# Gated mix of two linear-attention blocks on one core: the gate column made by VectorE, one block of copies moved to ScalarE

## The chip, the core and the metric

The kernel runs on one core of a Trainium2 chip. The time is the device time of one execution in microseconds, the median of several runs. The profile comes from one further execution. In it PE is TensorE, PEld TensorE's weight loads, DVE VectorE, ACT ScalarE, POOL GpSimd, and SP the engine that here only issues DMAs.

## The reference

Two linear-attention blocks, A and B, work on the same x (2048 x 640, bf16) with weights of their own, and a gate per row mixes them. Cut to what matters:

```python
x = A_x
g = sigmoid((x * gate_w).sum(-1, keepdims=True))
a = block(x, A_wqkv, A_wo)
b = block(x, B_wqkv, B_wo)
return g * a + (1 - g) * b

def block(x, wqkv, wo):              # 32 heads of 20
    q, k, v = split(x @ wqkv)
    pq, pk = phi(q), phi(k)          # phi(t) = (t + 1 if t > 0 else exp(t)) + 1e-6
    kv, z = pk.T @ v, pk.sum(rows)   # per head
    return ((pq @ kv) / (pq @ z + 1e-6)) @ wo
```

The row sums behind the gate are a matrix product of x with one column, gate_w. The kernel takes them from TensorE as one more column of block A's K product.

## The kernel before, in words

x is needed transposed (`xT`, 128 partitions x 5 chunks x 2048 rows), because TensorE contracts over partitions. Rows 512 to 2047 are transposed by DMA (L171). The first 512 rows come in as four blocks of 128 (`xn`, L151) and are transposed by TensorE in `x_transpose` (L249): five 128x128 transposes into PSUM, then two VectorE copies into `xT`, of chunks 0 and 1 and of chunks 2 to 4 (L255).

Block A's K weights lie in `wkA`, 128 x 5 x 642. Columns 0 to 639 of each chunk come by DMA (L154), and column 640 holds the gate weights. gate_w comes by DMA as five rows of 128 (`g5`, L160) and has to stand as one column of 128 for each chunk. `gate_column` (L222) does that: one TensorE transpose of `g5` into a corner of the PSUM tile that the warm-up used, and three ScalarE copies into column 640 (L227). `k_mm` (L295) reads 320 columns for the first half of the K product and 321 for the second half, so the gate's sum falls into column 320 of the second half's PSUM bank. `k_done` (L302) takes its exponential into `gl` (L305).

The order is written out by hand (`tc.manual_schedule()`, L943); every engine takes its instructions in the order of the program. Ahead of it stand seven warm-up matmuls on constants (L211). `k_first` (L318) runs the first four blocks:

1. transposes of block 0, transposes of block 1, the gate column;
2. eight kA matmuls with chunks 0 and 1: block 0 twice, block 1 twice (320 columns), then block 0 twice, block 1 twice (321 columns);
3. transposes of block 2, four kA matmuls with chunk 2, transposes of block 3, and then the rest of blocks 0 to 3.

Before `k_first`, SP issues in this order: x block 0, chunk 0 of wkA, `g5`, chunk 2 of wkA, chunks 3 and 4, the Q weights, the DMA transposes. ACT's queue issues x block 1, chunk 1 of wkA, x blocks 2 and 3, and then ACT loads its function table. VectorE begins with three small memsets (L142 to L144). GpSimd builds masks and identities for about the first 11 us (L176 to L203); among them is E4, part of `zE`, by memsets (L191, L192) and eight affine selects (L196).

PSUM tiles are handed out in four slots. `x_transpose` uses slots 3, 1, 0 and 1 for blocks 0 to 3, and the kA tiles of blocks 0, 1 and 2 use slots 2, 3 and 0. So block 1's kA tile takes the slot of block 0's transposes, and block 2's transposes take the slot of the warm-up tile.

Behind these come the other rows of K and Q of block A, then block B, the products of K with x and the output products. All of it is bound by TensorE and not touched by the change. The exponentials and the max of `phi` are `Phi` (L257): ACT's L266, then DVE's L274 and L285.

Of the kernel before, what the change touches and what calls it, by code (L numbers as in the profile page):

```python
# [9 lines left out]
P = 128  # L10
FP32 = mybir.dt.float32
BF16 = mybir.dt.bfloat16
# [3 lines left out]
S, D, H = 2048, 640, 32  # L16
Dh = D // H
DT = D // P
# [3 lines left out]
HB = 512  # L22
# [11 lines left out]
def kernel(  # L34
# [11 lines left out]
    nc = tc.nc  # L46
# [4 lines left out]
    persist = ctx.enter_context(tc.tile_pool(name="persist", bufs=1))  # L51
# [24 lines left out]
    def ps_raw(name, slot=None):  # L76

        if slot is None:
            slot = turn[0]
            turn[0] = (slot + 1) % 4  # L80
        return pools.get(slot, pools["ps"]).tile([P, 4 * HB], BF16, tag=f"ps{slot}", name=name)
# [5 lines left out]
    def ps(name, slot=None):  # L87

        return banks(ps_raw(name, slot))

    xT = persist.tile([P, DT, S], BF16, name="xT")
# [7 lines left out]
    ident = persist.tile([P, P], BF16, name="ident")  # L99
# [7 lines left out]
    lift = persist.tile([P, 1], FP32, name="lift")  # L107
    tiny = persist.tile([P, 1], FP32, name="tiny")
    ones = persist.tile([P, H], BF16, name="ones")
    g5 = persist.tile([DT, P], BF16, name="g5")  # L110
    gl = persist.tile([P, ST], FP32, name="gl")
    gf = persist.tile([P, 2, ST], FP32, name="gf")
    hc, ic = ST // 2, 2 * P
# [25 lines left out]
    wo_dram = [A_wo, B_wo]  # L139


    nc.vector.memset(ones[:], 1.0)  # L142
    nc.vector.memset(lift[:], 1.0 + EPS)
    nc.vector.memset(tiny[:], LOGS * EPS)  # L144
    xb0 = x2[0:CB * P, :].rearrange("(p q) d -> p q d", q=CB)
    wk = [None, None]
# [3 lines left out]
    def load_x(eng, lo, hi):  # L150
        eng.dma_start(out=xn[:, lo:hi, :], in_=xb0[:, lo:hi, :])  # L151

    def load_wk(eng, lo, hi):
        eng.dma_start(out=wk[0][:, lo:hi, 0:D], in_=wq_dram[0][:, lo:hi, D:2 * D])  # L154
# [2 lines left out]
    load_x(nc.scalar, 1, 2)  # L157
    load_wk(nc.sync, 0, 1)
    load_wk(nc.scalar, 1, 2)
    nc.sync.dma_start(out=g5[:], in_=gate_w.rearrange("(c p) -> c p", p=P))  # L160
    load_x(nc.scalar, 2, 3)
    load_wk(nc.sync, 2, 3)
    load_x(nc.scalar, 3, 4)
# [5 lines left out]
    for n in range(1, NB):  # L169
        for c in range(DT):  # L170
            nc.sync.dma_start_transpose(  # L171
                out=xT[:, c, n * HB:(n + 1) * HB], in_=x2[n * HB:(n + 1) * HB, c * P:(c + 1) * P]
# [4 lines left out]
    for r in range(4):  # L177
        rows = slice(32 * r, 32 * r + 32)
        nc.gpsimd.tensor_copy(out=I4[rows], in_=ident[rows, rows])
    nc.gpsimd.tensor_copy(  # L180
        out=spread[:].rearrange("p (h t) -> p h t", t=TW), in_=I4[:, :, None].to_broadcast([P, H, TW])
    )
    nc.gpsimd.memset(maskE[:], 1.0)
    for lo in range(0, HF, K6):
        part = maskE[:, lo:min(lo + K6, HF)]
        for sign, base in ((1, 0), (-1, Dh - 1)):
            nc.gpsimd.affine_select(
                out=part, in_=part, pattern=[[-sign * Dh, part.shape[1] // Dh], [0, Dh]],
# [4 lines left out]
    for r in range(4):  # L193
        rows, n = slice(32 * r, 32 * r + 32), HF if r < 2 else D
        for sign, base in ((1, 0), (-1, Dh - 1)):
            nc.gpsimd.affine_select(  # L196
                out=E4[rows, 0:n], in_=E4[rows, 0:n], pattern=[[sign, n]],
# [9 lines left out]
    warm_raw = ps_raw("warm", 0)  # L207
# [11 lines left out]
                    start=(c == 0), stop=(c == DT - 1), tile_position=(0, 32 * j),  # L219
                )  # L220

    def gate_column(pt):  # L222

        at = slice(4 * HB - 2 * P, 4 * HB - 2 * P + DT)
        nc.tensor.transpose(out=pt[:, at], in_=g5[:], identity=ident[0:DT, 0:DT])
        for lo, hi in ((0, 1), (1, 2), (2, DT)):
            nc.scalar.copy(out=wk[0][:, lo:hi, D:D + 1], in_=pt[:, at, None][:, lo:hi])  # L227

    def gate_rows():

# [18 lines left out]
    def x_transpose(i, slot):  # L249
        pt = ps_raw("xt", slot)  # L250
        for c in range(DT):
            nc.tensor.transpose(out=pt[:, c * P:(c + 1) * P], in_=xn[:, i, c * P:(c + 1) * P], identity=ident[:])  # L252
        src = pt[:, 0:D].rearrange("p (c n) -> p c n", c=DT)
        for lo, hi in ((0, 2), (2, DT)):
            nc.vector.tensor_copy(out=xT[:, lo:hi, i * P:(i + 1) * P], in_=src[:, lo:hi])  # L255

    class Phi:  # L257

# [36 lines left out]
    def k_mm(b, i, c, pt, hf):  # L295
        n = HF + (b == 0 and hf == 1)
        nc.tensor.matmul(  # L297
            pt[:, hf, 0:n], lhsT=xT[:, c, i * P:(i + 1) * P], rhs=wk[b][:, c, hf * HF:hf * HF + n],
            start=(c == 0), stop=(c == DT - 1),
        )  # L300

    def k_done(b, i, pt, lifted=False, between=None):  # L302
        f = Phi(pk[:, i, :].rearrange("p (b n) -> p b n", b=2), pt[:, :, 0:HF], lifted)
        if b == 0:
            nc.scalar.activation(out=gl[:, i:i + 1], in_=pt[:, 1, HF:HF + 1], func=ACT.Exp)  # L305
        f.clamp()
        if between is not None:
            between()
        f.top()

    def k_chunk(b, i, slot=None, lifted=False, between=None):
        pt = ps(f"k{'AB'[b]}", slot)
        for hf in range(2):
            for c in range(DT):
                k_mm(b, i, c, pt, hf)
        k_done(b, i, pt, lifted, between)

    def k_first():  # L318

        pts = []  # L320

        def part(i, cs, hfs=(0, 1)):
            for c in cs:
                for hf in hfs:
                    k_mm(0, i, c, pts[i], hf)

        x_transpose(0, 3)
        x_transpose(1, 1)
        gate_column(warm_raw)
        pts += [ps("kA", 2), ps("kA", 3)]  # L330
        for hf in range(2):
            for i in range(2):
                part(i, (0, 1), (hf,))
        x_transpose(2, 0)
        for i in range(2):
            part(i, (2,))
        x_transpose(3, 1)
        pts.append(ps("kA", 0))
        part(2, (0, 1, 2))
        for i in range(3):  # L340
            part(i, (3, 4))
            k_done(0, i, pts[i])
        k_chunk(0, 3, 1)
# [598 lines left out]

    with tc.manual_schedule():  # L943
        k_first()
        turn[0] = 2
        for n in range(2):
# [8 lines left out]
        for n in range(1, NB):  # L955
            nc.sync.dma_start(
                out=xn[:, n * CB:(n + 1) * CB, :], in_=x2[n * HB:(n + 1) * HB, :].rearrange("(q p) d -> p q d", p=P)
# [162 lines left out]
        for i in range(1, half):  # L1120
            p, after = pairs[i], pairs[i + 1] if i + 1 < half else None
# [49 lines left out]
```

## Time and profile before

| what | us |
|---|---|
| median of 3 runs | 183.86 |
| lowest and highest run | 183.67, 184.18 |
| profiled execution, its own time | 184.02 |
| its span, first to last instruction | 182.3 |
| PE busy | 178.1 |
| DVE busy | 148.3 |
| ACT busy | 109.0 |
| POOL busy | 9.5 |

How to read the profile: a timeline row gives start and length in us, the engine, the line in the kernel, the operation, output<-input, shapes, and how many instructions it merges. In brackets stand the idle time of the engine ahead of it and what ended it. A group row gives busy us and mean ns of one, then idle us. A row of the chain of waits gives start, length, and what held the end at that time. Starts are counted from the first instruction of the span.

### The profile page before, as it was taken

Reading aid. Unit: us, or ns where it says so; the run is one execution under the profiler, and the core shown is the slowest. Engines: PE = TensorE matmul, PEld = TensorE weight load, DVE = VectorE, ACT = ScalarE, POOL = GpSimd, SP = SyncE. Lnnn points to the kernel's source line nnn. Section 1 sums busy time; section 2 is a strip of 40 time slices with the busy share of each in tenths; the row PEclk is TensorE's granted clock in tenths of the full one; section 3 lists DMA queues with packets and bytes.
Section 4 is the critical chain, followed back from the end, with each engine's and each line's share of the span. In section 5 each row is a group of like instructions: output and inputs, shape, how many; then the busy total and the mean of one; then the engine's idle time right before and its main releaser. Section 6 shows DMA issues by size and latency. Waiting matters only on the chain.

```text
span 182.3 us, 3394 instructions
## 1 busy us (share of the span) xinstructions
PE 178.1 (98%) x1279; PEld 118.9 (65%) x1289; DVE 148.3 (81%) x268; ACT 109.0 (60%) x210; POOL 9.5 (5%) x30
## 2 busy tenths in 40 slices
PE   8999999999999999999999999999999999999993
PEld 4666656655666667676666665775678777777772
DVE  0468988999999799799898987979797987786854
ACT  2066579976884551795869596964814746464210
POOL 8930000000000000000000000000000000000000
PEclk9999999999999999999999999999999999999999
DMA  5984448974107200005000000053900740321232
GB/s 176 325 147 90 93 108 281 361 157 137 43 4 207 91 0 4 0 0 180 4 2 0 0 4 2 2 151 96 279 16 20 220 125 0 111 108 74 76 124 91
DMA packets 20494, 17.80 MB, mean 98 GB/s; under 512 B 9182, under 2 KB 19966, under 8 KB 20478
## 3 DMA queue, kind: packets, MB, share of 16 engines
q1 hardware_dynamic: 19534, 16.36, 31.1%
q10 hardware_dynamic: 944, 1.23, 2.2%
q8 instruction: 10, 0.16, 0.4%
q14 instruction: 6, 0.05, 0.1%
HBM read 11.34 MB, written 4.28 MB: 86 GB/s over the span
## 4 chain that ended last, share of the span: by engine, by line
PE 97%; DVE 1%; issue 0%
PE gs L517 17%; PE kA L297 13%; PE kB L297 12%; PE q L415 11%; PE qA L350 7%; PE oy L758 6%; PE oz L758 5%; PE ox L758 4%; PE ow L758 4%; PE q L350 2%; PE gB L487 2%; PE gA L487 2%; PE warm L211 2%; PE qB L350 1%; PE mA L648 1%; PE xt L252 1%
## 5 line engine op out<-in xcount | busy, mean ns | idle before, releaser
L297 PEld LDWEIGHTS <-xT 128*128 128x128 bf16 x320 | 31.2, 98 | 15.3 <-DVE xT L255 0.2
L274 DVE TENSOR_SCALAR e<-e 128x640 bf16<-128x640 bf16 (+2 forms) x58 | 19.7, 341 | 5.7 <-ACT e L266 5.2
L297 PE MATMUL kB<-wkB,xT 128*128 128x320 bf16 x160 | 24.2, 299 | 0.0
L297 PE MATMUL kA<-wkA,xT 128*128 128x320 bf16 (+1 forms) x160 | 23.9, 305 | 0.1
L266 ACT ACTIVATE e<-q 128x512 bf16<-128x512 f32 x26 | 15.7, 603 | 5.0 <-PE q L415 3.9
L517 PEld LDWEIGHTS <-xn 128*128 128x128 bf16 x128 | 12.2, 98 | 6.0 <-issue 1.3
L266 ACT ACTIVATE e<-kA 128x640 bf16<-128x640 f32 x16 | 11.3, 713 | 8.0 <-PE kA L297 7.9
L266 ACT ACTIVATE e<-kB 128x640 bf16<-128x640 f32 x16 | 11.4, 710 | 7.5 <-PE kB L297 7.3
L350 PE MATMUL qA<-xT,wqA 128*128 128x512 bf16 x57 | 13.3, 379 | 0.2
L350 PEld LDWEIGHTS <-wqA 128*128 128x128 bf16 x64 | 7.5, 117 | 5.9
L285 DVE SCALAR_TENSOR_TENSOR pk<-kB,e 128x640 bf16<-128x640 f32 x12 | 9.9, 822 | 1.0
L821 ACT COPY u<-ox 128x320 f32<-128x320 f32 x8 | 3.4, 425 | 11.9 <-PE ox L758 11.9
L758 PEld LDWEIGHTS <-xT 128*128 128x128 bf16 x85 | 8.1, 98 | 2.9
L758 PEld LDWEIGHTS <-pqTA 128*128 128x128 bf16 x85 | 8.0, 98 | 2.8
L763 DVE TENSOR_TENSOR osb<-oz,u 128x320 bf16<-128x320 f32 (+2 forms) x18 | 8.0, 453 | 2.3 <-PE oz L758 1.8
L758 PEld LDWEIGHTS <-pqTB 128*128 128x128 bf16 x80 | 7.8, 98 | 3.0
L517 PE MATMUL gs<-pk,xn 128*128 128x320 bf16 x64 | 9.4, 300 | 0.0
L285 DVE SCALAR_TENSOR_TENSOR pk<-kA,e 128x640 bf16<-128x640 f32 x10 | 8.2, 822 | 0.9
L433 DVE TENSOR_TENSOR q<-q,p 128x512 f32<-128x512 f32 x12 | 8.3, 692 | 0.8 <-PE q L415 0.6
L266 ACT ACTIVATE e<-qA 128x1024 bf16<-128x1024 f32 x6 | 6.2, 1027 | 4.2 <-PE qA L350 3.9
L487 PEld LDWEIGHTS <-xn 128*128 128x128 bf16 x64 | 6.3, 98 | 3.0
L517 PEld LDWEIGHTS <-S 128*128 128x128 bf16 x64 | 6.0, 98 | 2.6 <-issue 0.5
(189 smaller groups left out, 353.8 us busy)
## 6 DMA issues: line engine op xcount, KB each, us to landing
out_dram<-osb SPq DMA_DIRECT2D x14, 160.0 KB, 1.8
xn<-in_A_x_dram SPq DMA_DIRECT2D x3, 640.0 KB, 5.3
wvA<-in_A_wqkv_dram SPq DMA_DIRECT2D x1, 800.0 KB, 9.6
wkB<-in_B_wqkv_dram SPq DMA_DIRECT2D x1, 800.0 KB, 4.4
wqB<-in_B_wqkv_dram SPq DMA_DIRECT2D x1, 800.0 KB, 6.0
MA<-m_rows SPq DMA_DIRECT2D x1, 800.0 KB, 5.7
wqA<-in_A_wqkv_dram SPq DMA_DIRECT2D x2, 320.0 KB, 5.0
wvB<-in_B_wqkv_dram SPq DMA_DIRECT2D x2, 320.0 KB, 3.3
```

The lines of the kernel that those rows point to most:

```text
L211: nc.tensor.matmul(warm[:, 0, 0:n], lhsT=one_l, rhs=one_r[:, 0:n], start=True, stop=True)
L266: nc.scalar.activation(out=to, in_=part, func=ACT.Exp)
L274: nc.vector.tensor_scalar(self.e, self.e, 1.0, EPS, op0=ALU.min, op1=ALU.add)
L285: nc.vector.scalar_tensor_tensor(out=dst, in0=src, scalar=1.0 + EPS, in1=e, op0=ALU.add, op1=ALU.max)
L297: nc.tensor.matmul(pt[:, hf, 0:n], lhsT=xT[:, c, i * P:(i + 1) * P], rhs=wk[b][:, c, hf * HF:hf * HF + n], start=(c == 0), stop=(c == DT - 1),
L350: nc.tensor.matmul(dst, lhsT=mixed(wq[b][:, c, :], m), rhs=xT[:, c, n * HB:(n + 1) * HB], start=first, stop=last,)
L415: nc.tensor.matmul(dst, lhsT=left(c), rhs=right(c), start=first and k == 0, stop=k == len(cs) - 1, skip_group_check=not first,)
L433: nc.vector.tensor_tensor(out=dst, in0=src, in1=sb, op=ALU.add)
L487: nc.tensor.matmul(pt[:, hf, 0:HF], lhsT=xn[:, i, c * P:(c + 1) * P], rhs=pk[:, i, hf * HF:(hf + 1) * HF], start=(i == 0), stop=(i == ST - 1),
L517: nc.tensor.matmul(pt[:, n, 0:HF], lhsT=left[:, i, n * P:(n + 1) * P], rhs=right[:, i, :], start=(first and i == 0), stop=(i == hc - 1), s ...
L758: nc.tensor.matmul(dst, lhsT=left[:, c, r0:r0 + P], rhs=right[:, c, :], start=(first and c == 0), stop=(c == DT - 1), skip_group_check=not ...
L763: nc.vector.tensor_tensor(out=dst, in0=acc, in1=sb, op=ALU.add)
```

## The change

The gate column is made by VectorE and SBUF alone. `g5` gets 32 rows, zeroed by a memset on VectorE ahead of the DMA that fills rows 0 to 4. One VectorE transpose in blocks of 32 by 32 turns `g5` into `gT`: chunk c of gate_w's partitions 32g to 32g+31 then lies in column 32g + c. Four VectorE copies of 32 x 5 put these pieces into column 640 of `wkA`, one for each group of 32 partitions. The TensorE transpose and the three ScalarE copies are gone. The two copies behind the transposes of x's block 1 go from VectorE to ScalarE. On VectorE the gate's five instructions stand between the copies of block 0 and those of block 2.

```diff
-    g5 = persist.tile([DT, P], BF16, name="g5")
+    g5 = persist.tile([H, P], BF16, name="g5")
+    gT = persist.tile([H, P], BF16, name="gT")
...
+    nc.vector.memset(g5[:], 0.0)
     nc.vector.memset(ones[:], 1.0)
...
-    nc.sync.dma_start(out=g5[:], in_=gate_w.rearrange("(c p) -> c p", p=P))
+    nc.sync.dma_start(out=g5[0:DT], in_=gate_w.rearrange("(c p) -> c p", p=P))
...
-    def gate_column(pt):
-
-        at = slice(4 * HB - 2 * P, 4 * HB - 2 * P + DT)
-        nc.tensor.transpose(out=pt[:, at], in_=g5[:], identity=ident[0:DT, 0:DT])
-        for lo, hi in ((0, 1), (1, 2), (2, DT)):
-            nc.scalar.copy(out=wk[0][:, lo:hi, D:D + 1], in_=pt[:, at, None][:, lo:hi])
+    def gate_column():
+
+        nc.vector.transpose(out=gT[:], in_=g5[:])
+        for g in range(4):
+            rows = slice(H * g, H * g + H)
+            nc.vector.tensor_copy(out=wk[0][rows, :, D:D + 1], in_=gT[:, H * g:H * g + DT].rearrange("p (c o) -> p c o", o=1))
...
         for lo, hi in ((0, 2), (2, DT)):
-            nc.vector.tensor_copy(out=xT[:, lo:hi, i * P:(i + 1) * P], in_=src[:, lo:hi])
+            (nc.scalar.copy if i == 1 else nc.vector.tensor_copy)(out=xT[:, lo:hi, i * P:(i + 1) * P], in_=src[:, lo:hi])
...
         x_transpose(1, 1)
-        gate_column(warm_raw)
+        gate_column()
```

Two waits elsewhere follow from it. SP's issue of `g5` waits for the memset on VectorE, and the later load of block B's K weights into the place of `wkA` (L864) waits for VectorE's gate copies in place of ScalarE's.

## The prediction, made before the changed kernel was run

> **What bounds the kernel now.** I read the page first, then the chain of waits over the first 12 us, then the timeline of the stretch that the change touches. On the page PE is busy for 178.1 of 182.3 us, and PE carries 97% of the chain that ended last.
>
> ```profile
> span 182.3 us, 3394 instructions
> ...
> PE 178.1 (98%) x1279; PEld 118.9 (65%) x1289; DVE 148.3 (81%) x268; ACT 109.0 (60%) x210; POOL 9.5 (5%) x30
> ...
> PE 97%; DVE 1%; issue 0%
> ```
>
> So what counts is when PE can go on. Whatever moves PE's place at 7 us moves the end by nearly as much, because nothing later on PE waits for a transfer that would swallow the shift. The change sits wholly ahead of that place. The chain of waits there:
>
> ```profile
> 0.85 2.93 PE warm L211 x7
> 3.78 1.07 PE xt L252 x10
> 4.85 0.11 PE warm L225
> 4.96 1.92 PE kA L297 x8
> ...
> 7.99 3.84 PE kA L297 x28
> ```
>
> PE is on the chain without a break. The eight kA matmuls from 4.96 take 1.92 / 8 = 0.24 us each, the 28 from 7.99 only 3.84 / 28 = 0.137: PE is slow at first.
>
> The timeline of the stretch, in order of start; the 128x321 row holds the fifth to seventh kA matmul, the first that read the gate column. Under it stand the durations of all eight copies of L255 (shortest, median, longest), the shorter form 128x256 and the longer 128x384:
>
> ```profile
> 4.35 1.09 DVE L255 COPY xT<-xt 128x256 bf16<-128x256 bf16 x4 [3.35 <-PE xt L252]
> 4.56 0.61 DVE L255 COPY xT<-xt 128x384 bf16<-128x384 bf16 x2
> ...
> 4.78 0.10 PEld L225 LDWEIGHTS <-g 5*128 5x128 bf16 x1 [0.20 <-DMA g<-in_gate_w_dram]
> 4.89 1.99 PE L297 MATMUL kA<-wkA,xT 128*128 128x320 bf16 x8
> 5.00 0.30 ACT L227 COPY wkA<-warm 128x1 bf16<-128x1 bf16 x3 [1.01 <-PE warm L225]
> 5.23 1.32 PEld L297 LDWEIGHTS <-xT 128*128 128x128 bf16 x6 [0.21 <-DVE xT L255]
> 5.93 0.81 PE L297 MATMUL kA<-wkA,xT 128*128 128x321 bf16 x3
> 6.72 0.44 PE L252 MATMUL xt<-ident,xn 128*128 128x128 bf16 x5
> ```
>
> ```profile
> L255 DVE COPY xT<-xt x8: 290/320/348, 4.4 to 8.2; 128x256 bf16<-128x256 bf16 x4, 128x384 bf16<-128x384 bf16 x4
> ```
>
> The paces can be read from the starts. The first four kA matmuls take 5.93 - 4.89 = 1.04 us, 0.26 each. The next four take until the transposes at 6.72, 0.79 us, which is two at 0.26 and two at 0.137. So PE runs at half pace up to about 6.45 and at full pace from there. Time lost ahead of 6.45 costs half of itself, time lost behind it all of itself.
>
> **Part one: the gate transpose leaves PE.** The weight load for it waited 0.20 us for the DMA of g, to 4.78, and kA began at 4.89. Without it the first kA matmul waits for the first copy of block 0, which ends at 4.35 + 0.29 = 4.64, and for its weights (the last number of the first two rows is us from issue to landing):
>
> ```profile
> wkA<-in_A_wqkv_dram ACTq DMA_DIRECT2D x1, 160.0 KB, 3.2
> wkA<-in_A_wqkv_dram SPq DMA_DIRECT2D x1, 160.0 KB, 2.9
> ```
>
> ```profile
> 1.26 0.46 ACTq L154 DMA_DIRECT2D wkA<-in_A_wqkv_dram  x1
> 1.27 0.42 SPq L154 DMA_DIRECT2D wkA<-in_A_wqkv_dram  x1
> ```
>
> They land at 1.26 + 3.2 = 4.46 and 1.27 + 2.9 = 4.17. With 0.05 us for the release, kA starts at 4.69, 0.20 us earlier, and does the two matmuls of block 0 by about 5.2.
>
> **Part two: block 1's copies go to ACT.** The third kA matmul (block 1) needs the first of them. PE ends the transposes at 4.85 (chain). DVE began this copy at 4.56 + 0.61 - 0.29 = 4.88; ACT, idle at that time (1.01 us in its row above), begins at 4.89. A 128x256 copy of ACT out of PSUM isn't in the trace. The nearest rows of the groups (busy us, mean ns of one):
>
> ```profile
> L697 ACT ACTIVATE rT<-d 128x256 bf16<-128x256 f32 x4 | 1.6, 417 | 0.3
> L821 ACT COPY u<-ox 128x320 f32<-128x320 f32 x8 | 3.4, 425 | 11.9 <-PE ox L758 11.9
> ```
>
> It lies between 0.29 (as fast as DVE) and 0.42; I take 0.40, near ACT's rows. The copy ends at 5.29, and with the 0.06 us that the weight load needed behind it before (4.88 + 0.29 = 5.17, load at 5.23) the third kA matmul starts at 5.35; before, the third started two paces of 0.27 behind 4.89, about 5.40. Of the 0.20 us gained 0.05 is left. The fourth follows at 5.61, the fifth could start at 5.86 instead of 5.93. ACT's second copy ends at about 5.7; ACT's next work is the exponential of kA's first finished tile, several matmuls later, so nothing waits behind it. The three small copies that ACT loses cost nothing before.
>
> **Part three: the gate column on DVE.** The fifth kA matmul (128x321) needs all four copies into wkA. DVE can take the transpose after block 0's second copy: it starts where block 1's copy started before, 4.88 (g has landed by 4.78). Neither a 32x32-block transpose nor a 32x5 copy is in the trace; the nearest rows for their durations are these:
>
> ```profile
> L231 DVE TENSOR_SCALAR gf<-gl 128x16 f32<-128x16 f32 x1 | 0.2, 167 | 0.0
> ```
>
> ```profile
> 0.94 0.06 DVE L144 MEMSET tiny<- 128x1 f32 x1
> ```
>
> For the transpose of 128 elements per partition the bounds are 0.06 (the memset) and 0.35 (the 128x384 copy of L255); I take 0.29, its 128x256 copy. It ends at 5.17 and releases the first copy at 5.21. A copy of five elements takes between 0.06 and 0.17; I take 0.16 and no overlap, near the upper end, because the 16-element row reads SBUF as the copies do. Undisturbed the four end between 5.45 and 5.85, just ahead of the 5.86 at which PE asks. So what decides is whether they run undisturbed, and POOL is at work beside them:
>
> ```profile
> 5.06 0.36 POOL L192 MEMSET zE<- 64x320 bf16 x1
> ...
> 5.38 0.44 POOL L196 TENSOR_SCALAR_AFFINE_SELECT zE<-zE 32x320 bf16<-32x320 bf16 x1
> 5.88 0.44 POOL L196 TENSOR_SCALAR_AFFINE_SELECT zE<-zE 32x320 bf16<-32x320 bf16 x1
> 6.39 0.44 POOL L196 TENSOR_SCALAR_AFFINE_SELECT zE<-zE 32x320 bf16<-32x320 bf16 x1
> 9.71 0.72 POOL L196 TENSOR_SCALAR_AFFINE_SELECT zE<-zE 32x640 bf16<-32x640 bf16 x1
> 10.14 0.47 DVE L274 TENSOR_SCALAR e<-e 128x640 bf16<-128x640 bf16 x1 [1.56 <-ACT e L266]
> 11.50 0.32 DVE L274 TENSOR_SCALAR e<-e 128x640 bf16<-128x640 bf16 x1
> ```
>
> The last three rows are the evidence. DVE's eight copies out of PSUM all ran beside POOL at their even 290 to 348 ns. But the first DVE instruction that both reads and writes SBUF while POOL works, at 10.14, took 0.47 where the next of its kind took 0.32. Its last 0.32 began at 10.29: it stood 0.15 us, until 0.58 after POOL's start at 9.71, some 0.14 ahead of POOL's recorded end. So one kind of DVE instruction waits for POOL's running one, and the new copies are of its kind: one input, from SBUF to SBUF. By this row POOL holds DVE off during 5.06 to 5.28, 5.38 to 5.68, 5.88 to 6.18, 6.39 to 6.69. The first copy then runs 5.28 to 5.44, the second 5.68 to 5.84, the third right behind it to 6.00 (it comes ahead of POOL's 5.88, which starts when the copy is done and holds to 6.30), the fourth 6.30 to 6.46. PE sees the column at 6.5.
>
> The Trainium skill, SBUF — State Buffer, section "Who interferes with whom", says that DVE and GpSimd share one pair of SBUF ports, held by one instruction for its whole length, and that a DVE copy takes that pair in its two-port modes, for which the VectorE page (VectorE: DVE Perf Modes, "What auto-detection actually checks") asks for source and destination in SBUF with outer counts even or equal; here both are five. The trace agrees in the one case that it has, 0.47 against 0.32. By that rule the copies wait; a copy outside those modes would not.
>
> **The sum.** Before, the fifth kA matmul began at 5.93 and the next transposes at 6.72. Now the fifth begins at 6.5, when full pace has come; four at 0.137 end at 7.05. PE is 7.05 - 6.72 = 0.33 us late, say 0.3, and stays so. The other edits are hidden: the new memset on DVE stands ahead of three of which the last ended at 0.94 + 0.06 = 1.0, and SP's issue of g, which now waits for it, was at 1.74:
>
> ```profile
> 1.74 0.36 SPq L160 DMA_DIRECT2D g<-in_gate_w_dram  x1
> ```
>
> DVE's next copies, of block 2, wait for PE's transposes at 6.72 or later. POOL is pushed back by less than 4 x 0.17 us, in a total of 9.5 us of work for the whole span. The later load of wkB now waits for DVE's copy instead of ACT's, both long past.
>
> The profiled execution took 184.02 us, 1.72 more than its span; the median of the runs is 183.86, 0.16 less. The shift is added to the median: 183.86 + 0.33 = **184.2**.
>
> **Rivals.**
> *Undisturbed copies* (24%): DVE's small copies don't wait for POOL, or fit in its gaps. The column is there by 5.85, PE's fifth matmul starts at 5.86, 0.07 us early at half pace, and 0.03 is left at the end: 183.8. For it: one row alone shows the wait, and the copies are tiny. Against it: that row.
> *Every copy waits for a whole POOL instruction* (22%): if POOL's hold lasts to its recorded end and POOL always goes next, the copies run at 5.42, 5.82, 6.32 and 6.83, the column is there at 7.0, and PE's four matmuls end at 7.04 + 0.55 = 7.59: 0.87 late, 184.7. This is slower; it decides from a column at about 6.7 on, where PE is 0.55 late.
> *Full pace comes later* (13%): the row of the slow stretch, by engine:
>
> ```profile
> 4.90:5.90 1.00, 1.00 (x5) 0.53 (x5) 0.54 (x3) 0.30 (x3) 0.94 (x5) 1.00 1.06 380
> ```
>
> The chain shows full pace 5.6 us after the first warm matmul (0.85 to 6.45), with PE hardly idle. Now PE stands from about 5.87 to 6.5. If that pause makes the count begin again at 6.5, PE is at half pace until 12.1 and loses half of 5.6 us: 2.8 + 0.3, up to 187.0. The Trainium skill (TensorE: Matmul & The Clock Gate, Part 1) has such a gate, which judges whole windows of 3.4 us; by an estimate from that page one window more costs 1.7 + 0.3 us, 185.9. The trace can't confirm a clock: its granted clock (behind POOL's count in the row) reads 1.00 in the slow stretch too, so only the paces bear on it.
> *Faster* (7%): the gap of 0.2 us on PE ahead of 4.78 goes; if full pace then came at 4.9 instead of 6.45 and the column were in time, half of 1.5 us would be gained: 183.1. Nothing in the trace shows that so small a gap holds it back.
>
> **How the numbers follow.** The forecast has 34%, of which 4 lie past 0.3% (0.55 us); that bound is about what a measurement of this kernel can tell from no change. Faster 0.07; same 0.30 + 0.24 = 0.54; slower 0.04 + 0.22 + 0.13 = 0.39. The range takes in undisturbed copies and whole waits, with 0.3 us for the spread of the runs shown on both sides, and leaves out 0.20: 183.5 to 185.0. The forecast's own range is 184.0 to 184.5.
>
> **What would show it.** Right: the first kA matmul at 4.7, the third near 5.35, 32x5 copies on DVE that last or stand apart longer than 0.17 us where POOL is busy, PE waiting for wkA from DVE for about 0.6 us ahead of the first 128x321, the next transposes at about 7.05. Wrong: four copies done by 5.8 with no wait of PE; an ACT copy above 0.45 us, which makes the third matmul the late one; a transpose above 0.5 us, which makes the column late without POOL; a slow pace that lasts beyond 7 us.

## The result, and the profile after

| what | before | after |
|---|---|---|
| median, us | 184.05 | 184.42 |
| lowest and highest run | 183.29, 184.70 | 184.29, 186.64 |
| runs | 22 | 22 |
| profiled execution, its own time | 184.02 | 184.62 |
| its span | 182.3 | 182.9 |

The medians differ by 0.37 us. The ratio after to before is 1.0030, 95% interval 1.0016 to 1.0044; it is worked out from all runs and isn't the quotient of the two medians, which is 1.0020. Taken as time it is 0.55 us (0.29 to 0.81). So after is slower, and the size is known no better than that. The median of before shown at the start was that of the first three of these 22 runs.

The page of after. TensorE's share and the chain look as before; only the total tells that TensorE stood longer.

```profile
span 182.9 us, 3396 instructions
...
PE 178.3 (97%) x1278; PEld 118.6 (65%) x1288; DVE 149.3 (82%) x272; ACT 109.5 (60%) x209; POOL 9.7 (5%) x30
```

The chain of waits of after, first 12 us (start, length, what held the end). Before, PE was on it without a break from 0.85 on. Now it leaves PE at 4.33 and comes back at 6.45, by way of VectorE's gate column, instruction by instruction:

```profile
3.78 0.55 PE xt L254 x5
4.33 0.02 issue
4.35 0.24 DVE xT L257
4.59 0.24 issue
4.82 0.30 DVE gT L226
5.12 0.02 issue
5.15 0.31 DVE wkA L229
5.46 0.01 issue
5.47 0.40 DVE wkA L229
5.87 0.01 issue
5.88 0.17 DVE wkA L229
6.05 0.01 issue
6.07 0.34 DVE wkA L229
6.40 0.04 issue
6.45 0.83 PE kA L299 x4
```

Four copies of the same 32 x 5 elements take 0.31, 0.40, 0.17 and 0.34 us. The timeline of after shows what ran on GpSimd beside them (rows of three stretches):

```profile
5.08 0.36 POOL L194 MEMSET zE<- 64x320 bf16 x1
5.39 0.44 POOL L198 TENSOR_SCALAR_AFFINE_SELECT zE<-zE 32x320 bf16<-32x320 bf16 x1
5.91 0.45 POOL L198 TENSOR_SCALAR_AFFINE_SELECT zE<-zE 32x320 bf16<-32x320 bf16 x1
```

The first copy (5.15 to 5.46) lies beside the memset that ends at 5.44, the second (5.47 to 5.87) beside the select that ends at 5.83, the fourth (6.07 to 6.41) beside the one that ends at 6.36. Each slow copy is done 0.02 to 0.05 us after GpSimd's instruction. The third, the fast one, started in the gap between 5.83 and 5.91. The wait for GpSimd doesn't appear as idle time of VectorE but as a longer instruction.

The timeline of after for TensorE and ScalarE:

```profile
4.70 1.33 PE L299 MATMUL kA<-wkA,xT 128*128 128x320 bf16 x4
4.88 0.75 ACT L257 COPY xT<-xt 128x256 bf16<-128x256 bf16 x2 [0.90 <-PE xt L254]
5.31 0.40 PEld L299 LDWEIGHTS <-xT 128*128 128x128 bf16 x3 [0.48 <-ACT xT L257]
6.45 0.83 PE L299 MATMUL kA<-wkA,xT 128*128 128x321 bf16 x4 [0.42 <-DVE wkA L229]
7.12 0.44 PE L254 MATMUL xt<-ident,xn 128*128 128x128 bf16 x5
```

The bracket on the 128x321 row is the new wait. The fifth kA matmul began at 5.93 before and at 6.45 now, the transposes of block 2 at 6.72 and now at 7.12: TensorE is 0.40 us late. How far this lasts can be read from an instruction of VectorE that comes late in the kernel. First before, then after (shortest, median, longest ns, then first and last start):

```profile
L701 DVE TENSOR_TENSOR pqTA<-pqTA,pqTB x4: 815/818/824, 143.7 to 165.7; 128x1280 bf16<-128x1280 bf16 x4
```

```profile
L703 DVE TENSOR_TENSOR pqTA<-pqTA,pqTB x4: 816/818/825, 144.1 to 166.3; 128x1280 bf16<-128x1280 bf16 x4
```

The 0.4 us stands unchanged at 144 us. By 166 us this one execution has lost 0.2 more: TensorE's weight loads stand 0.34 us for a transfer into `MB`, up to 150.70. Neither the profile of before nor the two later profiles of after have this wait, so the 0.6 us between the two spans is more than the change costs.

### The profile page after: what moved, and what is told of

The parts are those of the page before. It is cut to its first block, busy times and chain, and to the rows that moved or that the text cites. A ratio compares the mean times of both kernels' runs of the same rounds, so it can differ in the third digit from the quotient of the medians.

```text
span 182.9 us, 3396 instructions
## 1 busy us (share of the span) xinstructions
PE 178.3 (97%) x1278; PEld 118.6 (65%) x1288; DVE 149.3 (82%) x272; ACT 109.5 (60%) x209; POOL 9.7 (5%) x30
## 4 chain that ended last, share of the span: by engine, by line
PE 96%; DVE 1%; issue 1%
PE gs L519 17%; PE kB L299 12%; PE kA L299 12%; PE q L417 11%; PE qA L352 7%; PE oy L760 6%; PE oz L760 5%; PE ox L760 4%; PE ow L760 4%; PE q L352 2%; PE gB L489 2%; PE gA L489 2%; PE warm L213 2%; PE qB L352 1%; PE mA L650 1%; PE kvA L634 1%
```

## The experiments

The theory: VectorE's four copies are held by GpSimd's running instruction, the column is late, and TensorE stands for it. Rivals: the five VectorE instructions are too slow in themselves; ScalarE's slower copy of block 1 is what costs; TensorE's half-pace stretch is longer because it stands idle.

**GpSimd's work moved behind the column** (e1). The two memsets and eight selects of `zE` and the second identity go to a function called behind the gate column. Its first instruction reads the column, so it starts when that is there:

```diff
+    def pool_rest():
+        nc.gpsimd.tensor_copy(out=gs[:], in_=wk[0][:, :, D:D + 1].rearrange("p c o -> p (c o)"))
+        nc.gpsimd.memset(E4, 1.0)
...
         gate_column()
+        pool_rest()
```

> The changed kernel, but GpSimd's work on zE and on the second identity waits until the gate column is written (a small GpSimd copy of the column stands ahead of it), so that GpSimd is idle while VectorE makes the four 32x5 copies. Theory (the copies wait for GpSimd's running instruction): each copy takes 0.17 us as the undisturbed third one did, the column is done at about 5.8 instead of 6.39, TensorE waits less than 0.1 us for it, and the time is that of before or up to 0.1 us under it: ratio to before 0.999 to 1.001. Its runs spread as widely as those of before (183.3 to 184.7), with none held up at 184.3. Rival (a copy into another group of partitions is slow by itself): copies of 0.3 to 0.4 us again, ratio 1.002 to 1.003.

Measured: 184.62 us against 184.36 for the kernel before on the same chip, ratio 1.0011 (0.9999 to 1.0023). The copies, by the group of their line in this kernel, and TensorE's timeline:

```profile
L232 DVE COPY wkA<-gT x4: 167/168/169, 5.2 to 5.7; 32x5 bf16<-32x5 bf16 x4
```

```profile
4.73 0.80 PE L302 MATMUL kA<-wkA,xT 128*128 128x320 bf16 x4
5.94 0.71 PE L302 MATMUL kA<-wkA,xT 128*128 128x321 bf16 x4 [0.41 <-DVE wkA L232]
6.48 0.44 PE L257 MATMUL xt<-ident,xn 128*128 128x128 bf16 x5
9.34 2.89 PE L302 MATMUL kA<-wkA,xT 128*128 128x320 bf16 x20 [0.76 <-DMA wkA<-in_A_wqkv_dram]
```

With GpSimd quiet the four copies are alike, 167 to 169 ns, and the column is there by 5.9. So the difference between 167 and 399 ns is GpSimd's, and the instructions aren't slow in themselves. The wait of TensorE for the column is a miss, 0.41 us where under 0.1 was expected: TensorE did the first four kA matmuls in 0.80 us and not in 1.33, and asked sooner. Whether the time came back in full isn't shown either: the ratio is 1.0011, and its interval holds both 1 and 1.002. In this profile TensorE, at the transposes by 6.48, stands 0.76 us for the transfer of `wkA`'s chunks 3 and 4. It is the slowest of the 12 executions (185.12), so how much the others lost there is not shown.

**The four copies as reductions** (e2). The copies become reductions over an axis of length one; GpSimd is left alone:

```diff
-            nc.vector.tensor_copy(out=wk[0][rows, :, D:D + 1], in_=...)
+            nc.vector.tensor_reduce(out=wk[0][rows, :, D:D + 1].rearrange(...), in_=..., axis=X, op=ALU.max)
```

> The changed kernel with the four 32x5 copies written as a maximum over an axis of length one (same values), GpSimd's work left where it is. Theory (a copy from SBUF to SBUF takes a port that GpSimd holds; a reduction doesn't): 0.17 us each or a little more, column at 5.8 to 5.9, ratio to before 0.999 to 1.001. Rival (any VectorE instruction on SBUF waits for GpSimd): 0.3 to 0.4 us for those that meet a GpSimd instruction, column at 6.4, ratio 1.002 to 1.003. Second rival (slow by the partitions): 0.3 us each, also where GpSimd is idle.

Measured on the same chip: 184.44, ratio 0.9999 (0.9986 to 1.0011). The timeline of this kernel:

```profile
5.23 0.70 DVE L229 TENSOR_REDUCE wkA<-gT 32x5 bf16<-32x5 bf16 x4
5.39 1.96 POOL L198 TENSOR_SCALAR_AFFINE_SELECT zE<-zE 32x320 bf16<-32x320 bf16 x4
5.98 0.71 PE L299 MATMUL kA<-wkA,xT 128*128 128x321 bf16 x4 [0.37 <-DVE wkA L229]
```

GpSimd works through the whole stretch and the four pieces are done in 0.70 us all the same, against 1.25 for the copies in after. So not every instruction of VectorE on SBUF waits for GpSimd. The Trainium skill (SBUF — State Buffer, "Who interferes with whom") says that on trn2 a reduction has no mode with two ports and never contends with GpSimd, while a copy can; the times in the two traces agree with both halves. No run here shows the ports themselves.

**After and the reductions on one chip** (a3, e2b). The reductions had not been timed beside after so far, and on the chip of the first experiments the wait for chunks 3 and 4 could have covered a late column. No new edit: after as it is, and the reductions.

> The changed kernel once more, as the partner of the next run on one chip: e1 and e2 ran without it, on a chip where the DMA of chunks 3 and 4 of wkA landed so late that it may have covered a late column too. Theory: the wait for the column is 0.4 us in the profile, ratio to before 1.002 to 1.004.

> The kernel of e2 (the four copies as reductions, all else as in the changed kernel), on the same chip. Theory (GpSimd's hold of the port is what makes the changed kernel slower): four reductions of 0.17 us, column at 5.8 to 5.9, ratio to before 0.999 to 1.001, and 0.2% or more under its partner. Rival (the late column is hidden behind the landing of chunks 3 and 4 anyway, and something else in the change costs 0.3%): the same ratio as its partner, 1.002 to 1.004, with the column early.

Measured against before (184.08): after 184.46, ratio 1.0021 (1.0003 to 1.0040), runs from 184.26 to 184.79; the reduction 184.03, ratio 0.9996 (0.9974 to 1.0019), runs from 183.60 to 184.29. The two sets of 12 runs barely touch, and their medians are 0.43 us apart. TensorE's timeline, after first, then the reduction:

```profile
6.42 0.71 PE L299 MATMUL kA<-wkA,xT 128*128 128x321 bf16 x4 [0.51 <-DVE wkA L229]
6.97 0.44 PE L254 MATMUL xt<-ident,xn 128*128 128x128 bf16 x5
```

```profile
4.88 1.91 PE L299 MATMUL kA<-wkA,xT 128*128 128x320 bf16 x8
6.62 0.44 PE L254 MATMUL xt<-ident,xn 128*128 128x128 bf16 x5
```

In the second the eight kA matmuls are one unbroken group and the wait is gone; the transposes come 0.35 us earlier. The four instructions that write the column are the only difference between the two kernels, and with GpSimd quiet the copies take what the reductions take. So their hold by GpSimd is worth the whole loss of after, as far as these runs can tell: 0.43 us against 0.38.

**Each half of the change alone** (e3, e4). First the kernel before with block 1's copies on ScalarE, then the gate column of after with block 1's copies back on VectorE:

```diff
-            nc.vector.tensor_copy(out=xT[...], in_=src[:, lo:hi])
+            (nc.scalar.copy if i == 1 else nc.vector.tensor_copy)(out=xT[...], in_=src[:, lo:hi])
```

> One half of the change alone: block 1's two copies on ScalarE, the gate column by TensorE and ScalarE as before. Theory (only the late gate column costs): ScalarE ends its copies at 5.64 and the three small gate copies behind them at about 5.85, just ahead of the first matmul of 321 columns at 5.93; ratio to before 0.999 to 1.001. Rival (ScalarE's slower copy is what costs): third kA matmul late by 0.1 us or more against 5.40, ratio above 1.001.

```diff
-            (nc.scalar.copy if i == 1 else nc.vector.tensor_copy)(out=xT[...], in_=src[:, lo:hi])
+            nc.vector.tensor_copy(out=xT[...], in_=src[:, lo:hi])
```

> The other half alone: the gate column on VectorE behind block 1's copies, which stay on VectorE. Theory: the transpose starts 0.6 us later than in the changed kernel (at about 5.4 instead of 4.82), the copies end at 6.9 to 7.1, TensorE waits for the column until about 7.0, at full pace already; four matmuls of 0.137 end at 7.55 to 7.65, 0.85 to 0.95 us behind the 6.72 of before: ratio 1.004 to 1.006. If the wait of TensorE for the column were not what costs, it would be like the changed kernel, 1.003 or less.

Measured: ScalarE's copies alone 184.48, ratio 1.0004 (0.9989 to 1.0020); the gate column alone 185.57, ratio 1.0061 (1.0041 to 1.0081). The timeline of the gate column alone:

```profile
5.70 0.29 DVE L226 STREAM_TRANSPOSE gT<-g 32x128 bf16<-32x128 bf16 x1
6.03 1.03 DVE L229 COPY wkA<-gT 32x5 bf16<-32x5 bf16 x4
7.11 0.71 PE L299 MATMUL kA<-wkA,xT 128*128 128x321 bf16 x4 [1.06 <-DVE wkA L229]
7.65 0.44 PE L254 MATMUL xt<-ident,xn 128*128 128x128 bf16 x5
```

ScalarE's copies cost nothing that can be measured, and the reductions, which have them too, are level with before in the pair above; so that rival falls. In the gate column alone VectorE comes to the gate 0.88 us later (5.70 against 4.82), and TensorE's wait is 1.06 in place of 0.42. Not all of the 0.88 is block 1's copies: VectorE's first copy began 0.35 us later too in this execution (4.70 against 4.35). The two halves belong together. With ScalarE's copies the loss is about half (1.0030 for 1.0061), though the two ratios are from different chips.

**Both kernels on another chip** (b2, a2): one profiled execution of the kernel before, and after timed:

> The kernel before, unchanged, profiled on the chip of these runs. In the four experiments so far TensorE stood at a new place, the first kA matmul of chunk 3, until the DMA of chunks 3 and 4 of wkA landed (at 8.7 to 9.4 us, where the first profile of before shows a landing at 7.4). First theory (this DMA's landing is the next floor behind the gate column and differs from chip to chip or execution to execution): if it lands after about 8.5 here, TensorE stands for it in this profile too, with kA's chunk 3 starting at the landing. Rival (the experiments' own edits delay the DMA): it lands at 7.4 to 7.9 and TensorE doesn't stand.

> The changed kernel, unchanged, on the chip of these runs. Theory: the wait for the gate column is again about 0.4 us and the copies that meet GpSimd's instructions again take 0.3 to 0.4 us; TensorE reaches chunk 3 at about 9.05. Where the DMA of chunks 3 and 4 lands at 9.0 or later, that wait covers the late column, and the ratio to before falls to 0.999 to 1.002; where it lands before 8.6, the ratio is 1.002 to 1.004 as in the first measurement.

Measured: the profiled execution of before 184.16; after 184.60 against 183.83, ratio 1.0032 (1.0014 to 1.0051). The ratio is that of the result, and TensorE's wait for the column is 0.46 us in this profile of after. The timeline of the kernel before on this chip:

```profile
4.75 1.41 PE L297 MATMUL kA<-wkA,xT 128*128 128x320 bf16 x8
6.00 0.45 PE L252 MATMUL xt<-ident,xn 128*128 128x128 bf16 x5
```

Its eight kA matmuls took 1.41 us here and 1.99 in the profile that the prediction used: full pace came well before 5.9. Yet this execution took 184.16, the other 184.02. The transposes of block 2 came 0.72 us earlier (6.00 for 6.72), and the end did not. The expectation asked about the landing of chunks 3 and 4. They landed at about 3.7 + 4.3 = 8.0, between its two cases, and the weight loads stand 0.22 us up to 8.13 with no releaser in the profile; at the first Q matmul TensorE is 0.53 us ahead (11.13 for 11.66). (The expectation says that all four experiments stood for these chunks. The gate column alone did not.) The rest went in two waits of the weight loads that the first profile of before doesn't have:

```profile
16.24 4.75 PEld L297 LDWEIGHTS <-xT 128*128 128x128 bf16 x36 [0.41 <-DMA xT<-in_A_x_dram]
150.23 1.20 PEld L758 LDWEIGHTS <-pqTB 128*128 128x128 bf16 x10 [0.39 <-DMA MB<-m_rows]
```

The first is for a block of x that DMA transposes, and behind it TensorE is 0.27 us ahead (21.16 for 21.43). The second is for the transfer into `MB`, and behind it nothing is left. An early place at 7 us is no gain where later transfers don't come earlier too.

**Block 2 transposed while the column is made** (e5, e6, e9). The five transposes go ahead of the 321-column matmuls, in after, in before, and in the kernel with the reductions:

```diff
-        x_transpose(2, 0)
...
+            if hf == 0:
+                x_transpose(2, 0)
```

> The changed kernel with the five transposes of x's block 2 moved ahead of the four matmuls that read the gate column. Theory: TensorE has work while the column is late; it waits for it 0.1 us or not at all, and the matmuls of 321 columns start at about 6.4; in front of chunk 3 TensorE is 0.4 us earlier than in the changed kernel, as early as before. Ratio to before 0.998 to 1.001. Rival (the loss is not in the wait for the column): like the changed kernel.

> The kernel before with the same move as in e5: the five transposes of x's block 2 ahead of the four matmuls that read the gate column. In the kernel before the column was never waited for, so theory says that the move gains nothing here: ratio 0.999 to 1.001, or up to 0.3 us slower where block 2's data land later than 5.9 and TensorE stands for them. Rival (the move itself is what helped e5): ratio 0.997 to 0.999.

> The changed kernel with both mends: the four copies as reductions, and block 2's transposes ahead of the matmuls that read the column. Theory: no wait for the column is left, and what remains of the change is TensorE's freed 0.1 us, most of it ahead of full pace or swallowed by the landing of chunks 3 and 4 of wkA: ratio 0.998 to 1.001, so no gain over the kernel before that 0.3% could show. If the freed slot on TensorE were worth its full 0.2 us in every execution: 0.998 or 0.999 with an interval under 1.

Measured: in after 184.24 against 183.83, ratio 1.0011 (0.9993 to 1.0028); in before 184.10 against 183.72, 1.0013 (0.9995 to 1.0031); with the reductions 184.18 against 183.72, 1.0024 (1.0008 to 1.0040). The timeline of after with the move:

```profile
5.93 0.45 PE L254 MATMUL xt<-ident,xn 128*128 128x128 bf16 x5
6.45 1.26 PE L299 MATMUL kA<-wkA,xT 128*128 128x321 bf16 x8
```

TensorE hardly waits for the column any more: the transposes fill the time up to 6.38, and 0.07 us is left. About two thirds of after's ratio went with the wait, though the intervals overlap. With the reductions there was nothing left to cover, and the move alone made before no faster. That the kernel with both came out slower than before is a miss, and its cause stays open. Its profiled execution (183.84) is the second fastest of the 12 and can't show what the others lost: none of TensorE's matmuls waits in the first 20 us but the first of the warm-up, and at the first Q matmul it is 0.47 us ahead of before (11.19 for 11.66). One possible price of the move is that it asks for block 2's data sooner than they land. The weight loads of the moved transposes, in after with the move, did stand for them:

```profile
5.92 0.28 PEld L254 LDWEIGHTS <-xn 128*128 128x128 bf16 x5 [0.35 <-DMA xn<-in_A_x_dram]
```

There TensorE had the matmuls ahead to do until 5.92, so this wait cost it next to nothing. That it costs more where full pace comes early is argued and not shown.

**Chunks 2 to 4 of `wkA` in one transfer** (e7), on the kernel with the reductions, against TensorE's wait for chunks 3 and 4 seen above:

```diff
-    load_wk(nc.sync, 2, 3)
+    load_wk(nc.sync, 2, DT)
...
-    load_wk(nc.sync, 3, DT)
```

> The changed kernel with the four copies as reductions (which don't meet GpSimd) and chunks 2 to 4 of wkA in one DMA, issued at about 2.2 us where chunk 2 alone was (chunks 3 and 4 were issued at 3.72, behind the landing of x's block 0). Theory (the next floor is the landing of chunks 3 and 4): they land at about 7 us, TensorE no longer stands at chunk 3, and executions whose full pace comes early gain up to 1 us: ratio 0.994 to 0.998, under both kernels. Rival (the DMA engines are full, so an earlier issue lands no earlier): ratio 0.999 to 1.001.

Measured: 186.31, ratio 1.0143 (1.0098 to 1.0188), a miss. TensorE's timeline in this kernel:

```profile
7.39 0.45 PE L253 MATMUL xt<-ident,xn 128*128 128x128 bf16 x5 [0.90 <-DMA xn<-in_A_x_dram]
9.06 0.71 PE L298 MATMUL kA<-wkA,xT 128*128 128x320 bf16 x4 [1.21 <-DMA wkA<-in_A_wqkv_dram]
```

The 480 KB, issued at 2.14, landed 6.9 us later, at 9.0, where 7 was expected. TensorE stood 0.90 us for block 2 of x, whose transfer now had the larger one beside it, and got chunk 2 only together with chunks 3 and 4 (1.21 us). So here an earlier issue of chunks 3 and 4 didn't bring them earlier than in before (3.7 + 3.7 = 7.4), and what TensorE needs first came later.

## Why the prediction was right, point by point

**The frame**, that TensorE's place at 7 us moves the end by nearly as much, held for after: +0.40 at 7.12, +0.4 at 144 us, +0.37 in the medians. Its reason, that nothing later on TensorE waits for a transfer, was true of the profile read but not of others: in the kernel before on the other chip two later transfers, at 16 and at 150 us, took back most of a gain. In other executions too the transfer of chunks 3 and 4 of `wkA` took longer. The rows of the DMA queues (KB, us from issue to landing), first of before, then of the kernel with the reductions in its first run:

```profile
wkA<-in_A_wqkv_dram SPq DMA_DIRECT2D x1, 320.0 KB, 3.7
```

```profile
wkA<-in_A_wqkv_dram SPq DMA_DIRECT2D x1, 320.0 KB, 5.3
```

There TensorE waited for it at 9.43. So a delay at 7 us reached the end, while a gain at 7 us was swallowed, in part or whole, by later landings. This also fits the first run of the reductions: transposes at 6.52 in place of 6.72, and a ratio of 0.9999.

**Part one.** The first kA matmul at 4.69: it came at 4.70.

**Part two.** ScalarE's first copy from 4.89 for 0.40: its pair of copies started at 4.88, and the group of its line gives 373 ns for the shorter and 485 for the longer form:

```profile
L257 ACT COPY xT<-xt x2: 373/429/485, 4.9 to 5.2; 128x256 bf16<-128x256 bf16 x1, 128x384 bf16<-128x384 bf16 x1
```

The weights behind it were loaded from 5.31, as 0.03 less in the copy makes it.

**Part three.** The transpose took 0.29 as taken, from 4.82 and not 4.88. Block 0's copies started at 4.35 and 4.56 in both profiles; what began at 4.88 before was a copy that needed block 1's transposes on TensorE, which ended at 4.85, and VectorE's transpose needs none of them. The copies' ends, forecast against measured: 5.44 and 5.46, 5.84 and 5.87, 6.00 and 6.05, 6.46 and 6.41. The step with most risk in it, that the third copy comes ahead of GpSimd's next select and the others wait until shortly before the recorded end of GpSimd's instruction, went as written, but for one point. The prediction had GpSimd's select start behind the third copy, at 6.00. It was recorded from 5.91, beside the copy, and took 0.45, hardly more than before (0.44). That is why the fourth copy was done at 6.41 and not at 6.46. An undisturbed copy is 0.17 long, one hundredth above the 0.16 taken. One row of before (0.47 against 0.32) carried this part, and it carried rightly. The same instruction in after, by the timeline, with GpSimd's select of 32x640 ending at 10.47, ahead of it, and GpSimd's next select beside it:

```profile
9.75 0.72 POOL L198 TENSOR_SCALAR_AFFINE_SELECT zE<-zE 32x640 bf16<-32x640 bf16 x1
10.54 0.33 DVE L276 TENSOR_SCALAR e<-e 128x640 bf16<-128x640 bf16 x1 [1.56 <-ACT e L268]
10.54 0.47 POOL masks.py:199 TENSOR_SCALAR_AFFINE_SELECT GT<-GT 128x128 f32<-128x128 f32 x1
```

It took 0.33: the slow first of its kind was GpSimd's doing. Five starts of it, between 10.04 and 10.26 in five profiles, fell beside the select that ends at 10.42 to 10.47 there: it took 0.57, 0.53, 0.51, 0.47 and 0.35, and was done at 10.61 to 10.66 each time. In after, where VectorE came at the same time as a new select, GpSimd's instruction was the longer one, 0.47 where the same one took 0.29 in before. So the hold was seen the other way round too; the prediction had it on VectorE's side and, for GpSimd, only as a delayed start.

**The sum.** The column was seen at 6.45 in place of 6.5, but the four matmuls to the transposes took 7.12 - 6.45 = 0.67 in place of 4 x 0.137 = 0.55. So the delay was 0.40 and not 0.33 in this profile. In the two other profiles of after they took the 0.55 (6.42 to 6.97 in the row above), so full pace, which the sum took to be there by 6.5, came slightly later in this execution. The forecast 184.2 and the measured 184.42 differ by 0.22, of which 0.19 is the other median of before (184.05 for 183.86). That the shift of 0.33 comes so near to the 0.37 of the medians is in part luck: at the transposes the three profiles of after are 0.40, 0.27 and 0.25 late against the one of before, the medians of the three comparisons differ by 0.37, 0.77 and 0.38, and the ratio of the result stands for 0.55.

**The rivals.** Undisturbed copies: didn't happen, but the reductions show what they would have given, 0.9996 and 0.9999 of before. Whole waits for GpSimd: the third copy ran in the gap, and a held one ends 0.02 to 0.05 us behind GpSimd's end, not a copy's length behind it. Full pace later: TensorE stood 0.42 us and went on at or near full pace. One of the 22 runs took 186.64, in that rival's range, with a mean granted clock of 0.99 where the others have 0.999 or 1.000; there is no profile of it, and it stays open. Faster: no, though full pace did come early in several profiles; the spread suggests, without showing it, that such an execution then only waits longer for the column: the lowest run of after was 184.26 to 184.31 in all three comparisons, that of before 183.21 to 183.60.

## What to carry to other kernels

Before moving work to VectorE, look at what GpSimd does in the same microseconds: here copies from SBUF to SBUF that take 0.17 us alone lasted until GpSimd's running instruction ended, 0.31 to 0.40 us, and the trace shows that as a longer instruction and not as a wait. If the piece is small and on the path, try a form that GpSimd doesn't hold (here a reduction over an axis of one, at the same 0.17 us), or move GpSimd's work. And when a wait is removed near the start of a kernel, look at which transfer is next in several profiles and not in one, because its landing may vary by more than the gain.

## What the runs showed that was not expected

- One 320 KB transfer landed 3.7 us after its issue in one of the two rows above and 5.3 in the other, and TensorE waited 0.76 and 0.81 us for it in the profiles of the first two experiments.
- TensorE reaches full pace at very different times for the same warm-up: the first four kA matmuls took 1.33 us in after (from 4.70) and 0.80 in the kernel with GpSimd's work moved (from 4.73), each with a wait for the weights of block 1 in it. The profile's granted clock reads 1.00 in both. The Trainium skill (TensorE: Matmul & The Clock Gate, Part 1) says that the gate's window runs freely and that the point of change differs from run to run; the paces agree, and no run here shows the gate itself.
- A copy of 32 x 5 elements costs 167 ns undisturbed, hardly more than a reduction's 165, and VectorE's transpose of 32 x 128 in 32 by 32 blocks 0.29 us, also beside GpSimd at work.
- No version tried beat the kernel before: the best, the reductions, gave 0.9996 (0.9974 to 1.0019) and 0.9999 (0.9986 to 1.0011).
